# Attention and a Mish layer on one core: weight loads in quarters, deeper input loads, and q/k transposed by DMA instead of TensorE

## The chip, the cores and the metric

The kernel runs on one core of one Trainium2 chip. The metric is the device time of one execution in microseconds (us); lower is better. Before the change it took 547.76 us (median of 3 runs, 545.96 to 547.79; with a fourth run, 547.60). Each run has a granted TensorE clock, the mean share of full speed that the throttle allowed, and a state: "fast" or "slow".

A *slot* in this text is the program's unit of work for one pair of heads: 8 batches of 6 pairs make 48 pairs, 0 to 47.

## The reference, cut to what matters

```python
# q, k, v: (8, 12, 448, 64) f32;  w_in: (768, 2048);  w_out: (2048, 768)
scores = scale * np.matmul(q, k.transpose(0, 1, 3, 2))
m = np.max(scores, axis=-1, keepdims=True)
e = np.exp(scores - m)
attn = e / (np.sum(e, axis=-1, keepdims=True) + np.exp(-m) + 1e-09)   # "softmax off by one"
x = (attn @ v), heads merged                      # 3584 tokens x 768
h = x @ w_in
out = (h * np.tanh(softplus(h))) @ w_out          # Mish between two matrix products
```

## The kernel before

The kernel gives q and k to TensorE with the head dimension on the partitions, so they are transposed. For each pair, SyncE issues seven loads, GpSimd casts to bf16, TensorE transposes against an identity into PSUM, and VectorE copies the result to SBUF. `x_pool` has two PSUM buffers, shared between these transposes and the two attention outputs of a pair.

```python
    stage = ctx.enter_context(tc.tile_pool(name="stage", bufs=3))    # f32 loads, three pairs deep
...
    def transposes(j):
        got = cast.pop(j)
        ps = x_pool.tile([128, 1024], BF16, tag="x", name="tr_ps")
        for i, name in enumerate(("q", "k")):
            mb, tb = got[name]
            for t in range(NT):                                      # NT = 3 blocks of 128 rows
                c = i * S + t * 128
                nc.tensor.transpose(ps[:, c : c + 128], mb[:, t]..., ident)
            c = i * S + MAIN                                         # then the tail of 64 rows
            nc.tensor.transpose(ps[:, c : c + TAIL], tb..., ident[0:64, 0:64])
        qk = work.tile([128, S + MAIN], BF16, tag="qk", name="qk")
        kt = k_tail[j % 2]
        nc.vector.tensor_copy(out=qk, in_=ps[:, 0 : S + MAIN])
        for h in range(2):
            r = slice(h * 64, h * 64 + 64)
            nc.vector.tensor_copy(out=kt[r, r], in_=ps[r, S + MAIN : 2 * S])
        qk_t[j] = qk
```

All weights (12.6 MB of f32, cast to bf16 on the way) are issued by GpSimd at the start. A slot then interleaves the attention of one pair with *units* of the two weight products of earlier batches: `mm1` is x times w_in (6 matmuls a unit), `mm2` is the gated result times w_out (8 matmuls a unit). They fill TensorE while ScalarE works on the softmax. After the fifth slot of a batch, ScalarE does the Mish of the batch before, and eight mm2 units keep TensorE busy meanwhile.

```python
        def slot(j, units):
            ...
            if j + 3 < J:
                load(j + 3)
            if j + 2 < J:
                do_cast(j + 2)
            rest = max(0, len(units) - 2)
            if j < J:
                scores(j, 0)
            take(1)
            if j + 1 < J:
                transposes(j + 1)
            take(1)
            if j >= 1:
                attend(j - 1)
            if j < J:
                scores(j, 1)
            take((rest + 1) // 2)
            if j >= 1:
                normalize(j - 1)
            take(len(units))
```

The softmax here doesn't subtract the row's maximum and nothing guards it: scores larger than these inputs give would overflow.

## Time and profile before

| | before |
|---|---|
| time, median of 3 | 547.76 us |
| span of the profiled execution | 546.4 us |
| TensorE busy, share of the span | 88% |
| ScalarE busy | 55% |
| first Mish starts | 113.0 us |
| last block of eight mm2 units under Mish starts | 463.5 us |

The page of the profiled execution, first its busy times, then busy tenths in 40 slices of 13.7 us (9 is 90% or more; PEclk is the granted clock), then two DMA queues with packets, MB and their share of 16 engines' time. Queue q1 is SyncE's, q0 is GpSimd's, which carries the weights.

```profile
PE 483.3 (88%) x2768; PEld 234.0 (43%) x2768; DVE 206.3 (38%) x414; ACT 297.9 (55%) x419; POOL 130.2 (24%) x400
PE   4354779948999799999999899999997999989996
PEclk9999869986999899999999899999999999989999
DMA  5999554200530434034511353035503420110012
q1 hardware_dynamic: 64768, 44.06, 28.8%
q0 software_dynamic: 2976, 6.29, 6.1%
```

TensorE is little used in the first four slices, where DMA stands at 9 from the second to the fourth, and nearly full from the seventh, but for a dip around the first Mish (slice 9). So the kernel has two regimes with different limits, and the overall 88% describes neither.

The chain of waits of the kernel before (start, length, what) between 14 and 48 us:

```profile
15.95 18.75 DMA km<-in_k_dram
34.76 12.81 DMA kt<-in_k_dram
```

For 31.6 us the chain is nothing but two k loads that queue among the weights. The same view in a slot that TensorE bounds:

```profile
279.77 0.65 PE s_ps L149 x4
280.41 1.24 PE h_ps L205 x6
281.65 0.17 PE tr_ps L125 x3
281.82 0.13 PE tr_ps L129
281.95 0.27 PE tr_ps L125 x3
282.23 0.13 PE tr_ps L129
282.36 1.24 PE h_ps L205 x6
...
287.79 0.33 PE o_ps L248 x2
```

The slot lasts from 279.77 to 287.79, 8.02 us. The four `tr_ps` pieces, the eight transposes of one pair, are 0.70 us of it.

### The profile page before, as it was taken

Reading aid. Unit: us, or ns where it says so; the run is one execution under the profiler, and the core shown is the slowest. Engines: PE = TensorE matmul, PEld = TensorE weight load, DVE = VectorE, ACT = ScalarE, POOL = GpSimd, SP = SyncE. Lnnn points to the kernel's source line nnn. Section 1 sums busy time; section 2 is a strip of 40 time slices with the busy share of each in tenths; the row PEclk is TensorE's granted clock in tenths of the full one; section 3 lists DMA queues with packets and bytes.
Section 4 is the critical chain, followed back from the end, with each engine's and each line's share of the span. In section 5 each row is a group of like instructions: output and inputs, shape, how many; then the busy total and the mean of one; then the engine's idle time right before and its main releaser. Section 6 shows DMA issues by size and latency. Waiting matters only on the chain.

```text
span 546.4 us, 7802 instructions
## 1 busy us (share of the span) xinstructions
PE 483.3 (88%) x2768; PEld 234.0 (43%) x2768; DVE 206.3 (38%) x414; ACT 297.9 (55%) x419; POOL 130.2 (24%) x400
## 2 busy tenths in 40 slices
PE   4354779948999799999999899999997999989996
PEld 1111224413445344555445444554453544535553
DVE  3012224622553245524553255434552365220121
ACT  3034464595567555765658556855577465752200
POOL 5413533230230323112420333013311330000000
PEclk9999869986999899999999899999999999989999
DMA  5999554200530434034511353035503420110012
GB/s 135 212 218 219 149 151 120 67 2 0 138 95 30 130 99 134 1 110 126 152 33 54 106 147 86 31 108 149 134 1 112 120 59 1 59 29 31 29 59 86
DMA packets 67783, 50.85 MB, mean 93 GB/s; under 512 B 24480, under 2 KB 63392, under 8 KB 67744
## 3 DMA queue, kind: packets, MB, share of 16 engines
q1 hardware_dynamic: 64768, 44.06, 28.8%
q0 software_dynamic: 2976, 6.29, 6.1%
q8 instruction: 21, 0.34, 0.3%
q14 instruction: 18, 0.15, 0.1%
HBM read 45.61 MB, written 11.01 MB: 104 GB/s over the span
## 4 chain that ended last, share of the span: by engine, by line
PE 82%; ACT 6%; DMA 6%; SPq 3%; DVE 1%; issue 1%; POOL 0%; POOLq 0%
PE o_ps L248 28%; PE h_ps L205 28%; PE av_ps L172 10%; PE s_ps L149 6%; PE tr_ps L125 4%; DMA km<-in_k_dram 3%; PE av_ps L181 3%; DMA kt<-in_k_dram 2%; PE tr_ps L129 2%; PE s_ps L161 2%; ACT e L156 2%; ACT ln L189 1%; ACT rc L190 1%; SPq L78 1%; ACT gm L233 1%
## 5 line engine op out<-in xcount | busy, mean ns | idle before, releaser
L205 PE MATMUL h_ps<-xT,w_in_sb 128*128 128x448 bf16 x768 | 164.7, 358 | 2.0 <-DVE xT L200 2.0
L189 ACT ACTIVATE ln<-av_ps 64x448 f32<-64x448 f32 x96 | 51.7, 539 | 172.9 <-PE av_ps L181 171.7
L156 ACT ACTIVATE e<-s_ps 128x896 bf16<-128x896 f32 x144 | 126.0, 909 | 22.5 <-PE s_ps L149 20.1
L248 PE MATMUL o_ps<-w_out_sb,gm 128*128 128x384 bf16 x768 | 134.9, 333 | 0.0
L213 DVE COPY h_sb<-h_ps 128x448 f32<-128x448 f32 x112 | 70.0, 625 | 97.0 <-PE h_ps L205 96.1
L205 PEld LDWEIGHTS <-w_in_sb 128*128 128x128 bf16 x768 | 71.2, 99 | 68.4 <-issue 12.0
L248 PEld LDWEIGHTS <-gm 128*128 128x128 bf16 x768 | 75.3, 99 | 53.0 <-issue 5.1
L200 DVE TENSOR_TENSOR xT<-av_ps,rc 64x448 bf16<-64x448 f32 x96 | 59.7, 622 | 74.9 <-ACT rc L190 72.6
L149 PE MATMUL s_ps<-qk 64*128 64x448 bf16 x288 | 52.8, 384 | 27.1 <-ACT e L156 26.1
L256 DVE COPY o_sb<-o_ps 128x384 f32<-128x384 f32 x56 | 31.2, 557 | 100.1 <-PE o_ps L248 99.5
L102 POOL CAST qmb<-qm 128x384 bf16<-128x384 f32 x48 | 24.4, 508 | 141.9 <-DMA qm<-in_q_dram 135.3
L134 DVE COPY qk<-tr_ps 128x832 bf16<-128x832 bf16 x48 | 28.4, 591 | 61.1 <-PE tr_ps L129 58.9
L233 ACT ACTIVATE gm<-h_sb 128x1536 bf16<-128x1536 f32 x28 | 39.2, 1470 | 0.1
L149 PEld LDWEIGHTS <-qk 64*128 64x128 bf16 x288 | 14.5, 96 | 52.2 <-issue 51.0
L125 PE MATMUL tr_ps<-ident,qmb 128*128 128x128 bf16 x144 | 17.9, 240 | 14.5 <-POOL qmb L102 14.5
L190 ACT ACTIVATE rc<-ln 128x448 f32<-128x448 f32 x48 | 27.7, 576 | 1.5
L102 POOL CAST kmb<-km 128x384 bf16<-128x384 f32 x48 | 24.3, 505 | 16.4 <-DMA km<-in_k_dram 16.2
L162 ACT ACTIVATE e<-s_ps 128x448 bf16<-128x448 f32 x48 | 25.7, 536 | 0.0
L125 PE MATMUL tr_ps<-ident,kmb 128*128 128x128 bf16 x144 | 18.1, 242 | 6.5 <-POOL kmb L102 6.5
L125 PEld LDWEIGHTS <-qmb 128*128 128x128 bf16 x144 | 12.2, 106 | 25.8 <-POOL qmb L102 16.1
L248 PE MATMUL o_ps<-w_out_sb,gt 128*128 128x384 bf16 x128 | 22.3, 326 | 0.0
L217 ACT ACTIVATE gm<-h_ps 128x384 bf16<-128x384 f32 x16 | 7.9, 491 | 25.7 <-PE h_ps L205 25.7
(58 smaller groups left out, 338.5 us busy)
## 6 DMA issues: line engine op xcount, KB each, us to landing
qm<-in_q_dram SPq DMA_DIRECT2D x48, 192.0 KB, 2.6
km<-in_k_dram SPq DMA_DIRECT2D x48, 192.0 KB, 2.7
vm<-in_v_dram SPq DMA_DIRECT2D x48, 192.0 KB, 2.7
out_dram<-o_sb SPq DMA_DIRECT2D x24, 384.0 KB, 2.7
w_in_sb<-in_moe_w_in_dram POOLq DMA_DIRECT2D x6, 512.0 KB, 11.5
w_out_sb<-in_moe_w_out_dram POOLq DMA_DIRECT2D x4, 768.0 KB, 26.9
qt<-in_q_dram SPq DMA_DIRECT2D x48, 32.0 KB, 2.6
kt<-in_k_dram SPq DMA_DIRECT2D x48, 32.0 KB, 2.8
```

What stands on the lines that cost most here:

```text
L102: nc.gpsimd.tensor_copy(out=mb.rearrange("p t h d -> p h t d"), in_=main)
L125: nc.tensor.transpose(ps[:, c : c + 128], mb[:, t].rearrange("p h d -> p (h d)"), ident)
L149: nc.tensor.matmul(sp[:, h, 0:S], lhsT=qk[r, S + t * 128 : S + (t + 1) * 128], rhs=qk[r, 0:S], start=True, stop=True,)
L156: nc.scalar.activation(out=e[:, 2 * t : 2 * t + 2, :], in_=sp[:, :, 0:S], func=AF.Exp, scale=SCALE)
L172: nc.tensor.matmul(av[h][:, 0:S], lhsT=va[:, 2 * t + h, :], rhs=e[:, 2 * t + h, :], start=(t == 0), stop=False,)
L189: nc.scalar.activation(out=ln[r, :], in_=av[h][o, 0:S], func=AF.Ln, bias=1.0)
L190: nc.scalar.activation(out=rc, in_=ln, func=AF.Exp, scale=-1.0)
L200: nc.vector.tensor_mul(x_t[b][r, hp, :], av[h][r, 0:S], rc[r, :])
L205: nc.tensor.matmul(hp[:, 0:S], lhsT=w_in_sb[:, dm, ff * 128 : (ff + 1) * 128], rhs=x_t[b][:, dm, :], start=(dm == 0), stop=(dm == DM_T - 1),)
L213: nc.vector.tensor_copy(out=h_sb[:, ff, :], in_=hp[:, 0:S])
L233: nc.scalar.activation(out=gm[:, f, :], in_=h_sb[:, f, 0:MAIN], func=AF.Mish)
L248: nc.tensor.matmul(op[:, 0:HALF], lhsT=lhs, rhs=w_out_sb[:, ff, n * HALF : (n + 1) * HALF], start=(ff == 0), stop=(ff == FF_T - 1),)
```

## The change

Its intent: take q/k transposes off TensorE for pairs 6 to 47, by a DMA that transposes from SBUF to SBUF; and let attention start while the weights come in, by loading them in quarters when slots need them. The rest serves these two: input loads four pairs deep, k and q in one tile (six blocks of 128 rows, then two tails), mm1 and mm2 units placed where TensorE idled. The core of the diff:

```diff
-    stage = ctx.enter_context(tc.tile_pool(name="stage", bufs=3))
+    stage = ctx.enter_context(tc.tile_pool(name="stage", bufs=4))
+    qk_pool = ctx.enter_context(tc.tile_pool(name="qk", bufs=4))
...
     def do_cast(j):
...
+        if j >= NPAIR:                      # NPAIR = 6
+            qk = qk_pool.tile([128, 2 * S], BF16, tag="qk", name="qk")
+            nc.sync.dma_start_transpose(
+                out=qk[:, 0 : 2 * MAIN].rearrange("p (t c) -> p t c", c=128),
+                in_=mb.rearrange("p t h d -> p (t h d)"),
+            )
+            nc.sync.dma_start_transpose(
+                out=qk[:, 2 * MAIN : 2 * S].rearrange("p (t c) -> p t c", c=TAIL),
+                in_=tb.rearrange("p t h d -> p (t h d)"),
+            )
+            qk_t[j] = qk
...
     def transposes(j):
+        if j >= NPAIR:
+            for h in range(2):
+                r = slice(h * 64, h * 64 + 64)
+                nc.gpsimd.tensor_copy(out=kt[r, r], in_=qk_t[j][r, S + MAIN : 2 * S])
+            return
+        for t in range(2 * NT):             # six blocks of 128 rows
+            nc.tensor.transpose(...)
+        for t in range(2):                  # then both tails
+            nc.tensor.transpose(...)
...
-        for dm in range(DM_T):              # all weights at the start
-            nc.gpsimd.dma_start(out=w_in_sb[:, dm, :], ...)
+        def load_w_in(i):                   # a quarter of the columns of w_in
+            c = slice(i * d_ff // 4, (i + 1) * d_ff // 4)
+            nc.gpsimd.dma_start(
+                out=w_in_sb[:, :, c], in_=moe_w_in[:, c].rearrange("(m p) f -> p m f", p=128)
+            )
...
-            if j + 3 < J:
-                load(j + 3)
+            if j + 4 < J:
+                load(j + 4)
             if j + 2 < J:
                 do_cast(j + 2)              # the DMA transposes are issued in here
+            if 1 <= j <= 4:
+                load_w_in(j - 1)
+            if 6 <= j <= 9:
+                load_w_out(j - 6)
...
+                late = p == 1 and i == 0    # two mm1 units at the end of slot 6
...
-        slot(J, [])
+        m2 = mm2_units(B - 2)
+        slot(J, m2[:4])                     # four mm2 units in the last slot
+        m2 = m2[4:]
```

More of the change, by code (lines that the diff above doesn't have):

```diff
@@ L97, in do_cast @@
         tiles = loaded.pop(j)
-        got = {}
-        for name in ("q", "k"):
+        mb = half.tile([128, 2 * NT, 2, D], BF16, tag="mb", name="mb")
+        tb = half.tile([64, 2, 2, D], BF16, tag="tb", name="tb")
+        for i, name in enumerate(("k", "q")):
             main, tail = tiles[name]
-            mb = half.tile([128, NT, 2, D], BF16, tag=f"{name}mb", name=f"{name}mb")
-            nc.gpsimd.tensor_copy(out=mb.rearrange("p t h d -> p h t d"), in_=main)
-            tb = half.tile([64, 2, D], BF16, tag=f"{name}tb", name=f"{name}tb")
-            nc.gpsimd.tensor_copy(out=tb, in_=tail)
-            got[name] = (mb, tb)
+            nc.gpsimd.tensor_copy(
+                out=mb[:, i * NT : (i + 1) * NT].rearrange("p t h d -> p h t d"), in_=main
+            )
+            nc.gpsimd.tensor_copy(out=tb[:, 1 - i], in_=tail)
         main, tail = tiles["v"]
@@ L115, in do_cast @@
             )
-        cast[j] = got
-    def transposes(j):
-        got = cast.pop(j)
-        ps = x_pool.tile([128, 1024], BF16, tag="x", name="tr_ps")
-        for i, name in enumerate(("q", "k")):
-            mb, tb = got[name]
-            for t in range(NT):
-                c = i * S + t * 128
-                nc.tensor.transpose(
-                    ps[:, c : c + 128], mb[:, t].rearrange("p h d -> p (h d)"), ident
-                )
-            c = i * S + MAIN
+        cast[j] = (mb, tb)
+        if j >= NPAIR:
[9 more added lines that the diff above has]
+            qk_t[j] = qk
+    def transposes(j):
+        mb, tb = cast.pop(j)
+        kt = k_tail[j % 2]
+        if j >= NPAIR:
[3 more added lines that the diff above has]
+            return
+        ps = x_pool.tile([128, 1024], BF16, tag="x", name="tr_ps")
+        for t in range(2 * NT):
             nc.tensor.transpose(
-                ps[:, c : c + TAIL], tb.rearrange("p h d -> p (h d)"), ident[0:64, 0:64]
+                ps[:, t * 128 : (t + 1) * 128], mb[:, t].rearrange("p h d -> p (h d)"), ident
             )
-        qk = work.tile([128, S + MAIN], BF16, tag="qk", name="qk")
-        kt = k_tail[j % 2]
-        nc.vector.tensor_copy(out=qk, in_=ps[:, 0 : S + MAIN])
+        for t in range(2):
+            c = 2 * MAIN + t * TAIL
+            nc.tensor.transpose(
+                ps[:, c : c + TAIL], tb[:, t].rearrange("p h d -> p (h d)"), ident[0:64, 0:64]
+            )
+        qk = qk_pool.tile([128, 2 * S], BF16, tag="qk", name="qk")
+        nc.vector.tensor_copy(out=qk[:, 0 : S + MAIN], in_=ps[:, 0 : S + MAIN])
         for h in range(2):
@@ L150, in scores @@
                     sp[:, h, 0:S],
-                    lhsT=qk[r, S + t * 128 : S + (t + 1) * 128],
-                    rhs=qk[r, 0:S],
+                    lhsT=qk[r, t * 128 : (t + 1) * 128],
+                    rhs=qk[r, MAIN : MAIN + S],
                     start=True,
@@ L160, in scores @@
             sp = s_pool.tile([128, 2, 512], FP32, tag="s", name="s_ps")
-            nc.tensor.matmul(sp[:, 0, 0:S], lhsT=kt, rhs=qk[:, 0:S], start=True, stop=True)
+            nc.tensor.matmul(sp[:, 0, 0:S], lhsT=kt, rhs=qk[:, MAIN : MAIN + S], start=True, stop=True)
             nc.scalar.activation(
@@ L280 @@
         nc.scalar.preload_act_table_set("natural_log_exp_and_others")
-        for j in range(3):
+        for j in range(4):
             load(j)
@@ L285, with load_w_out, slot, take @@
         do_cast(1)
-        for dm in range(DM_T):
+        def load_w_in(i):
+            c = slice(i * d_ff // 4, (i + 1) * d_ff // 4)
             nc.gpsimd.dma_start(
-                out=w_in_sb[:, dm, :], in_=moe_w_in[dm * 128 : (dm + 1) * 128, :]
+                out=w_in_sb[:, :, c], in_=moe_w_in[:, c].rearrange("(m p) f -> p m f", p=128)
             )
-        n = FF_T // 4
-        for i in range(4):
-            f = slice(i * n * 128, (i + 1) * n * 128)
+        def load_w_out(i):
+            n = FF_T // 4
             nc.gpsimd.dma_start(
                 out=w_out_sb[:, i * n : (i + 1) * n, :],
-                in_=moe_w_out[f, :].rearrange("(f p) c -> p f c", p=128),
-            )
-        def slot(j, units):
-            def take(n):
+                in_=moe_w_out[i * n * 128 : (i + 1) * n * 128, :].rearrange(
+                    "(f p) c -> p f c", p=128
+                ),
+            )
+        def slot(j, units, late=False):
+            def take(n, last=False):
+                if late and not last:
+                    return
                 for _ in range(min(n, len(units))):
                     units.pop(0)()
-            if j + 3 < J:
-                load(j + 3)
+            if j + 4 < J:
+                load(j + 4)
             if j + 2 < J:
                 do_cast(j + 2)
+            if 1 <= j <= 4:
+                load_w_in(j - 1)
+            if 6 <= j <= 9:
+                load_w_out(j - 6)
             rest = max(0, len(units) - 2)
@@ L320, in slot @@
                 normalize(j - 1)
-            take(len(units))
+            take(len(units), last=True)
         for p in range(B):
@@ L326 @@
             for i in range(NPAIR):
-                if i == 0:
+                late = p == 1 and i == 0
+                if late:
+                    units, m1 = m1[:2], m1[2:]
+                elif i == 0:
                     units, m2 = m2[:4], m2[4:]
@@ L332 @@
                     units, m2 = m2, []
-                slot(p * NPAIR + i, units)
+                slot(p * NPAIR + i, units, late)
                 if i == 4 and p >= 1:
@@ L338 @@
                         u()
-        slot(J, [])
+        m2 = mm2_units(B - 2)
+        slot(J, m2[:4])
+        m2 = m2[4:]
         m1 = mm1_units(B - 1, direct=True)
-        m2 = mm2_units(B - 2)
         while m1 or m2:
```

## The prediction

> **What bounds the kernel now (547.8 us; profiled span 546.4).** Three regimes, by the chain of waits and the table by stretches.
>
> 1. 0 to 79.5 us, pairs 0 to 6, no weight matmuls yet. From 16 to 48 us the DMA engines are saturated (share 1.11, 219 GB/s) by all weights, issued from 11.7 us on. They cost 6.1% of 16 engines' span, 33 us of full DMA time, and q/k/v loads queue behind them: the chain shows 18.75 us of `km` and 12.81 us of `kt`. Attention starts at 24.6, 37.6, 49.3, then every 8.2 us once the weights are in: a latency loop (scores, transposes, VectorE copy, attention, Ln, Exp) at a granted clock of 0.69.
> 2. 79.5 to 487 us: TensorE almost without gaps. In a full slot the eight transposes take 0.70 us of the chain.
> 3. In slots without filler (around the first Mish, and near 300, 418 and 480 us) TensorE waits on ScalarE; transposes plus the VectorE copies that release the second PSUM buffer cost about 2 us there. After the last attention TensorE waits 3 us (483.2 to 486.3).
>
> **What the change does.**
> - Weights: quarters issued in slots 1 to 4 and 6 to 9. A quarter is 33/8 = 4.2 us of DMA, a pair's loads 2.9 us (0.37 of 32 us for four pairs). 7.1 us fits in 8.2 us, so slots 1 to 6 should run at their latency. Estimate: slot 7 starts at 61 us, not 79.5: minus 18.
> - Transposes: 40 slots lose 0.70 us each: minus 28; unfilled slots lose 2 us: another 3.5. VectorE loses 42 copies of 591 ns and 84 of 184 ns; GpSimd (24% busy) gains 84 of some 0.2 us.
> - Two mm1 units (1.24 us each) fill idle time in slot 6: minus 2. Four mm2 units in the last slot: minus 2.6.
> - Added: two DMA transposes per pair on SyncE's queue, where seven load issues take 4.55 us. No trace here has a DMA transpose; the Trainium skill ("DMA: Bandwidth & Descriptors", Latency and other measured facts) gives 261 GB/s, so 230 KB are about 1 us of data, an estimate; issue I guess at 1 to 2 us each. That makes 6.5 to 8.5 us of queue per 7.3 us slot, below the batch mean of 9. They are issued about two slots before their scores, so latencies up to 8 us hide. The same page (Rules for kernel authors) says a transpose next to ordinary DMAs needs nothing.
>
> Sum: 18 + 31.5 + 4.6 = 54. I give back 1 us, and 6 more for contention in slots 1 to 10 and for stores that block SyncE ahead of transposes: **about 494 us**, range 481 to 512. Chances: faster by over 2% 0.95, within 2% 0.03, slower 0.02.
>
> **What would show each step.** The chain has no `km`/`kt` DMA pieces over 10 us; the first h_ps matmul comes at 52 to 64 us; DMA share is below 1 in slots 1 to 4. From slot 7 TensorE stays 95% busy, full slots last 7.3 instead of 8.0 us, and no TensorE wait names `qk` or `k_tail` released by a DMA. Six slots last about 54 instead of 58.6 us.
>
> **What would make it wrong.** DMA transposes that cost over 3 us each of SyncE's queue or over 8 us to land (scores then wait on `qk`, and slots follow the queue); w_out quarters plus transposes saturating the DMA in slots 6 to 9; weight quarters arriving after their mm1; ScalarE, 58% busy in full slots, becoming the limit.

## The result, and the profile after

The changed kernel takes 494.84 us (median of 4 runs, 491.99 to 498.20), against 547.60 us for the kernel before: a ratio of 0.9045, 95% interval 0.8969 to 0.9120. Ratios here and below are the mean time of one kernel's fast runs over that of the other's of the same rounds, so they are not quite the ratios of the medians. Executions over 1.5% slower than the fastest of the same kernel are left out of the means. All four runs fall in two groups, 492.0 and 492.3 at clocks of 0.965 and 0.960, and 497.4 and 498.2 at 0.947 and 0.943. The profiled run is the 497.4, so its trace shows the slower of the two groups, about 2.5 us above the median; what separates the groups, no trace here shows.

The page of the changed kernel, the same lines as before, and the shares of the chain of waits by engine:

```profile
PE 441.5 (89%) x2432; PEld 209.9 (42%) x2432; DVE 169.6 (34%) x288; ACT 297.9 (60%) x419; POOL 144.6 (29%) x482
PE   3677595828999899999998999999998999999995
PEclk9956697977999999999999999999999999999999
DMA  5699999951543464446453564365544620120112
q1 hardware_dynamic: 105088, 53.71, 42.8%
q0 software_dynamic: 5248, 6.29, 8.2%
PE 80%; DMA 7%; ACT 6%; SPq 3%; POOL 1%; issue 1%; DVE 0%; POOLq 0%
```

Three things stand out. The start is busier (TensorE row, slices 2 to 4), though slices 5 and 7 fall back to 5 tenths. The high DMA load now lasts to the eighth slice, about 99 us. And the weights, the same 12.6 MB, cost 8.2% of 495.6 us, 40.6 us of full DMA time, where they cost 6.1% of 546.4, 33.3 us, before. They come in 5,248 packets, not 2,976, because quarters of w_in's columns are cut into pieces of 1,024 bytes, not 4,096. But this is only half of it: by the packets in the two traces, w_in rose from 15.8 to 19.8 us, and w_out from 17.2 to 20.8 with the same 2,048 packets of 1,536 bytes. Why these took longer in slots 6 to 9, no run separates.

A full slot on the chain of waits of the changed kernel:

```profile
243.87 0.65 PE s_ps L165 x4
244.52 2.38 PE h_ps L221 x12
...
251.08 0.62 PE s_ps L165 x3
```

It lasts 7.21 us, 0.81 less: the 0.70 us of transposes are gone, and the two mm1 units that stood around them run without a break, in 2.38 us where they took 1.24 twice. VectorE's copies and their wait are gone as well.

Where the time came from, by three marks in the two profiled executions:

| mark | before | after | saved up to here |
|---|---|---|---|
| first Mish starts | 113.0 | 99.3 | 13.7 |
| last block of eight mm2 units under Mish starts | 463.5 | 416.2 | 47.3 |
| end | 546.4 | 495.6 | 50.8 |

So 13.7 us come from the first 11 slots, 33.6 from the next 36, most of which TensorE bounds, and 3.5 from the end.

But the first part is less than it should be. Scores of pair 7 start at 62.3 us in place of 79.1, 16.8 us earlier; by the first Mish, only 13.7 us are left, although four slots without transposes on TensorE lie between. The waits view (who waited for whom: us in total, times, longest) names what took it back:

```profile
PE s_ps L165 <- DMA qk<-tb: 9.4, 3, 5.2
PEld L165 <- DMA qk<-mb: 9.3, 2, 5.6
```

These are matmuls and their weight loads, waiting for transposes by DMA. In the timeline, the longest of them, with the issue of the transpose that it waited for:

```profile
71.18 1.18 SPq L125 DMA_TRANSPOSE qk<-tb  x1
...
81.81 0.93 PE L165 MATMUL s_ps<-qk 64*128 64x448 bf16 x4 [5.22 <-DMA qk<-tb]
```

This transpose landed 10.5 us after its issue; over the whole run the medians in the DMA issues view are 2.8 us (`qk<-mb`) and 2.3 (`qk<-tb`). It was also issued late: TensorE was ready for it at 76.6, only 5.4 us after its issue, although it stands two slots ahead in the program. And the wait cost more than its 5.2 us: the twelve h_ps matmuls after it took 4.66 us, where twelve take 2.43 just before the wait, at a granted clock of 0.50 from 81.8 to 87.4 us.

Busy time by stretches in the changed kernel, 32 to 48 and 62 to 82 us. The columns are stretch, length, busy time of TensorE, its weight loads, VectorE, ScalarE and GpSimd with counts, then granted clock, mean busy share of the DMA engines and GB/s. A share is the sum of the packets' times over the stretch, so it can exceed 1.

```profile
32.00:48.00 16.00, 11.31 (x43) 3.64 (x43) 3.76 (x10) 9.24 (x14) 7.38 (x22) 0.61 1.17 223
62.00:82.00 20.00, 14.51 (x80) 6.47 (x82) 7.50 (x13) 9.24 (x14) 7.37 (x23) 0.98 1.13 192
```

The DMA engines are saturated in both, in the second with TensorE idle for over a quarter of the time.

A second reading matters for what follows. SyncE's queue in a full slot of the changed kernel (start, length of the issue, line, what):

```profile
194.33 0.57 SPq L79 DMA_DIRECT2D qm<-in_q_dram  x1
194.96 0.66 SPq L91 DMA_DIRECT2D qt<-in_q_dram  x1
195.66 0.59 SPq L79 DMA_DIRECT2D km<-in_k_dram  x1
196.30 0.63 SPq L91 DMA_DIRECT2D kt<-in_k_dram  x1
196.97 0.59 SPq L79 DMA_DIRECT2D vm<-in_v_dram  x1
197.61 1.13 SPq L86 DMA_DIRECT2D vt<-in_v_dram  x2
198.85 1.25 SPq L121 DMA_TRANSPOSE qk<-mb  x1
200.20 1.17 SPq L125 DMA_TRANSPOSE qk<-tb  x1
201.43 0.57 SPq L79 DMA_DIRECT2D qm<-in_q_dram  x1
```

Nine issues take 7.10 us, back to back, in a slot of 7.21 us. In these slots the queue is full.

### The profile page after: what moved, and what is told of

The parts are those of the page before. It is cut to its first block, busy times and chain, and to the rows that moved or that the text cites. A ratio compares the mean times of both kernels' runs of the same rounds, so it can differ in the third digit from the quotient of the medians.

```text
span 495.6 us, 7105 instructions
## 1 busy us (share of the span) xinstructions
PE 441.5 (89%) x2432; PEld 209.9 (42%) x2432; DVE 169.6 (34%) x288; ACT 297.9 (60%) x419; POOL 144.6 (29%) x482
## 3 DMA queue, kind: packets, MB, share of 16 engines
q1 hardware_dynamic: 105088, 53.71, 42.8%
q0 software_dynamic: 5248, 6.29, 8.2%
## 4 chain that ended last, share of the span: by engine, by line
PE 80%; DMA 7%; ACT 6%; SPq 3%; POOL 1%; issue 1%; DVE 0%; POOLq 0%
PE o_ps L264 30%; PE h_ps L221 29%; PE av_ps L188 10%; PE s_ps L165 6%; DMA qk<-tb 3%; PE av_ps L197 3%; PE s_ps L177 2%; DMA vm<-in_v_dram 2%; ACT e L172 1%; ACT ln L205 1%; ACT gm L249 1%; DMA km<-in_k_dram 1%; DMA vt<-in_v_dram 1%; SPq L79 1%; ACT rc L206 1%
## 5 line engine op out<-in xcount | busy, mean ns | idle before, releaser
L221 PE MATMUL h_ps<-xT,w_in_sb 128*128 128x448 bf16 x768 | 158.6, 356 | 1.4 <-DVE xT L216 1.4
L264 PE MATMUL o_ps<-w_out_sb,gm 128*128 128x384 bf16 x768 | 132.0, 330 | 0.0
L221 PEld LDWEIGHTS <-w_in_sb 128*128 128x128 bf16 x768 | 73.4, 99 | 72.3 <-issue 11.2
L137 POOL COPY k_tail_97<-qk 64x64 bf16<-64x64 bf16 x42 | 9.8, 234 | 112.9 <-DMA qk<-tb 72.3
L137 POOL COPY k_tail_95<-qk 64x64 bf16<-64x64 bf16 x42 | 9.8, 234 | 76.3 <-DMA qk<-tb 48.2
L104 POOL CAST mb<-km 128x384 bf16<-128x384 f32 x48 | 24.2, 503 | 19.8 <-DMA km<-in_k_dram 17.2
L104 POOL CAST mb<-qm 128x384 bf16<-128x384 f32 x48 | 24.2, 503 | 0.0
L188 PE MATMUL av_ps<-e,v_aug_89 128*128 128x448 bf16 x72 | 18.0, 389 | 0.5 <-DVE k_tail_97 L153 0.5
L188 PE MATMUL av_ps<-e,v_aug_87 128*128 128x448 bf16 x72 | 18.0, 389 | 0.5 <-DVE k_tail_95 L153 0.5
```

Source lines behind the costliest of these rows:

```text
L104: nc.gpsimd.tensor_copy(out=mb[:, i * NT : (i + 1) * NT].rearrange("p t h d -> p h t d"), in_=main)
L188: nc.tensor.matmul(av[h][:, 0:S], lhsT=va[:, 2 * t + h, :], rhs=e[:, 2 * t + h, :], start=(t == 0), stop=False,)
L221: nc.tensor.matmul(hp[:, 0:S], lhsT=w_in_sb[:, dm, ff * 128 : (ff + 1) * 128], rhs=x_t[b][:, dm, :], start=(dm == 0), stop=(dm == DM_T - 1),)
L264: nc.tensor.matmul(op[:, 0:HALF], lhsT=lhs, rhs=w_out_sb[:, ff, n * HALF : (n + 1) * HALF], start=(ff == 0), stop=(ff == FF_T - 1),)
```

## The experiments

The total was as predicted, so the question is whether its parts were. The theory: (a) the start and the transposes are separate gains; (b) the first 11 slots lose some 8 us to a DMA overload; (c) SyncE's queue just keeps up. Rivals stand in each expectation.

### 1. The two halves alone

Weights, depth and fillers alone, every pair transposed by TensorE:

```diff
-        if j >= NPAIR:       # both places
+        if j >= J:
```

> Weight quarters, 4-deep loads and fillers, but every pair transposed by TensorE. Theory (the start and the transposes are two separate gains): slot 7 starts near 62 us as in the changed kernel, no TensorE wait names a DMA of qk, and each of the 42 pairs pays 0.8 to 1.0 us again: about 525 us, 20 to 25 us faster than before. Rival (the gain is nearly all transposes; early weight loading was hidden anyway): within 8 us of before, 540 or more.

Measured: 519.07 us, ratio 0.9512 (0.9456 to 0.9568). It is 6 us faster than expected. Slot 7 starts at 62.4 us, as expected. First Mish starts at 93.8 us, earlier than in the whole change (99.3), and no TensorE wait names a DMA of qk.

DMA transposes alone, with weights early, three-deep loads and no fillers, as in the kernel before:

```diff
-    stage = ctx.enter_context(tc.tile_pool(name="stage", bufs=4))
+    stage = ctx.enter_context(tc.tile_pool(name="stage", bufs=3))
...
-            if j + 4 < J:
-                load(j + 4)
+            if j + 3 < J:
+                load(j + 3)
...      (all weight loads ahead of slot 0; no "late" units; slot(J, []))
```

> DMA transposes of pairs 6 to 47 alone; weights early, loads 3-deep, no fillers, as before. Theory: slot 7 starts near 79 us as before, then about 1 us less per slot, 36 to 38 us in all: about 510 us. Rival (DMA transposes only pay with deeper loads, because SyncE's queue has no slack left): over 520 us, with TensorE or GpSimd waiting on loads or on qk in the full slots.

Measured: 506.23 us, ratio 0.9268 (0.9217 to 0.9318). Also faster than expected, and the rival falls: the transposes pay without deeper loads. Slot 7 starts at 74.0 us, not near 79 as expected, and the first Mish at 104.8 against 113.0. In the contended window of the other runs, 40 to 100 us, no transpose here took over 2.9 us to land.

The two ratios save 4.9% and 7.3%, together 12.2% or 66.8 us of 547.5. The whole change saves 9.55% or 52.3 us. So 14.5 us are lost when the two are put together, give or take some 6 us by the three intervals, and the next runs look for them.

### 2. A gain that was counted twice: the order of TensorE's transposes

The weights-only run had an unexpected detail. Its transposes take 0.50 us of a slot, not 0.70, although they are the same eight. The diff had also regrouped them: six blocks, then two tails. So this was done alone, in the kernel before:

```diff
         for i, name in enumerate(("q", "k")):
             mb, tb = got[name]
             for t in range(NT):
                 nc.tensor.transpose(...)        # three of 128 rows
+        for i, name in enumerate(("q", "k")):
+            mb, tb = got[name]
             c = i * S + MAIN
             nc.tensor.transpose(...)            # the tail of 64 rows
```

> The kernel before with one thing changed: a pair's eight TensorE transposes in the order six of 128 rows, then two of 64, not 3 + 1 + 3 + 1. The weights-only run shows 0.50 us of the chain for them, against 0.70 before. Theory: 0.20 us in each of some 40 slots that TensorE bounds: 8 us, 539 us. Rival (the 0.20 us came from the other edits of that run): within 2 us of before.

Measured: 537.70 us, ratio 0.9829 (0.9806 to 0.9852): 9.4 us from splitting one loop. A piece of its chain of waits:

```profile
257.53 1.24 PE h_ps L207 x6
258.77 0.34 PE tr_ps L125 x6
259.11 0.16 PE tr_ps L131 x2
259.27 1.24 PE h_ps L207 x6
```

Six take 0.34 us, where two groups of three took 0.17 and 0.27 before: the three blocks that followed a tail of 64 rows had cost 0.10 us more than the three that did not. The other 0.10 us comes from the tails, 0.16 us for both together where each took 0.13 alone. Why a change of shape costs TensorE this, no run here shows.

This gain is part of the weights-only run and cannot be had again once the transposes have left TensorE. It explains about 9 of the missing 14.5 us.

### 3. The overload of the first slots

By the queue shares, a quarter of the weights costs 40.6/8 = 5.1 us of full DMA time; a pair's loads 2.5 us; a pair's transposes (42.8% of 495.6 minus 28.8% of 546.4, over 42 pairs) 1.3 us. In slots 6 to 9 that makes 8.9 us in slots of 7.2 us. The loads are put here at the rate of q1 before the change, 44.06 MB in 28.8% of 546.4 us, 280 GB/s; the 2.9 us of the prediction and of an expectation below counts in an output store that ran in the same 32 us. Five runs attack this from different sides.

Loads three pairs deep again, all else as changed:

```diff
-            if j + 4 < J:
-                load(j + 4)
+            if j + 3 < J:
+                load(j + 3)
...      (stage bufs=3, three loads ahead of slot 0)
```

> The changed kernel with loads 3 deep instead of 4. Theory (depth only covers the longer landing times while weights are in flight): 2 to 8 us slower than the changed kernel, all lost before 110 us, full slots still 7.2 us. Rival (depth is what made the start faster): 12 us or more slower.

Measured: 490.94 us, ratio 0.8992 (0.8937 to 0.9047). Both theory and rival fail: it is not slower. First Mish starts at 90.6 us, 8.8 us earlier than in the changed kernel. Deeper loads do not help here.

The w_out quarters further apart:

```diff
-            if 6 <= j <= 9:
-                load_w_out(j - 6)
+            if j in (6, 8, 10, 11):
+                load_w_out((6, 8, 10, 11).index(j))
```

> The changed kernel with the w_out quarters in slots 6, 8, 10 and 11 instead of 6 to 9. Theory (5.1 us for a quarter plus 2.9 us of loads plus 1.3 us of transposes exceed a 7.2 us slot in slots 6 to 9): the 5.2 us wait of TensorE for qk at 82 us goes, first Mish near 93 us instead of 99, 5 to 8 us faster, near 488 us. Rival (the wait comes from the order of issue or from SyncE's queue, not from bytes): within 2 us of the changed kernel.

Measured: 491.74 us, ratio 0.9003 (0.8953 to 0.9052). This is 2 to 3 us better, inside the intervals, and less than expected. Where the theory looked it was right: pair 9 waits 0.6 us instead of 5.2, and the first Mish starts at 93.3 us. But TensorE's matmuls still wait 10.1 us in all for transposes, in other places, 3.8 us at 54 and 4.2 at 95. Fewer bytes per slot cure the wait they were aimed at, not the rest.

Four-deep loads kept, but each slot's transposes issued ahead of its loads:

```diff
-            if j + 4 < J:
-                load(j + 4)
             if j + 2 < J:
                 do_cast(j + 2)
+            if j + 4 < J:
+                load(j + 4)
```

> The changed kernel (4-deep loads) with each slot's two DMA transposes issued before its loads, not after them. On SyncE's queue this gives exactly the order of the 3-deep run, with the deeper buffers kept. Theory (a transpose lands late because one more pair of loads stands ahead of it in the queue): the 5.2 us wait on qk at 82 us goes, time within 3 us of the 3-deep run, near 490 us, and no slower. Rival (3-deep was better for another reason, such as fewer bytes in flight): within 2 us of the changed kernel, 494 us.

Measured: 489.72 us, ratio 0.8945 (0.8923 to 0.8967), a time as the theory said; the first Mish starts at 92.9 us. The wait got shorter and did not go, as the waits view shows:

```profile
PE s_ps L165 <- DMA qk<-tb: 5.2, 3, 2.7
PEld L165 <- DMA qk<-mb: 7.2, 3, 3.0
```

Between 40 and 100 us a transpose still landed up to 11.1 us after its issue, but was issued earlier, pair 6's at 39.9 us instead of 47.6. On SyncE's queue this order, T(j+2) L(j+4) T(j+3) L(j+5), is the same as the three-deep one, L(j+3) T(j+2) L(j+4) T(j+3), so depth as such is not what differs. In the order of the change, one more pair of loads stands ahead of each transpose, loads that nobody needs yet, and part of that time TensorE waits. Times alone are weak evidence here: the interval of this run and that of the changed kernel (0.8969 to 0.9120) only just part, and the three-deep run's overlaps both.

The two cures together:

> Transposes ahead of loads in each slot, and the w_out quarters in slots 6, 8, 10 and 11. Theory: the two cures act on the same wait, so they don't add: 1 to 3 us faster than transposes-first alone, 487 to 489 us, first Mish near 90 us. Rival (they add up, 2.6 and 5 us): 484 us or less.

Measured: 488.03 us, ratio 0.8934 (0.8911 to 0.8957). All four runs lie within 0.5 us, where the changed kernel's spread over 6 us. First Mish starts at 88.5 us, and no matmul waits for qk any more (3.9 us of weight-load waits remain). Stretch 62 to 82 us of this run, with the columns as above:

```profile
62.00:82.00 20.00, 20.00 (x110) 8.73 (x109) 10.07 (x18) 12.69 (x20) 9.39 (x31) 1.00 0.86 175
```

TensorE has no gap at all where it was busy 14.5 of 20 us, and DMA is below saturation. Whether the two cures add, the times do not tell: it is about 1 us over the order alone, within the intervals, and a full sum, 2 to 3 us more, would have given 487 us (the 484 of the rival counts more than that). In the profiled executions they nearly add: against 99.3 us, the first Mish starts 6.0 us earlier with the quarters spread, 6.4 with the order changed, 10.8 with both.

Last, no DMA transposes while w_out loads, by leaving pairs 6 to 11 to TensorE:

```diff
-        if j >= NPAIR:       # both places
+        if j >= 12:
```

> The changed kernel with pairs 6 to 11 transposed by TensorE too, so that no DMA transpose is in flight with the w_out quarters. Theory: six slots pay 0.6 us again in filled slots and about 2 us where nothing fills (some 5 us), and the waits on qk before 100 us (about 9 us of TensorE, and the low clock after) go: first Mish near 94 us as in the weights-only run, 488 to 492 us. Rival (waits on qk cost little in the end): slower than the changed kernel by 4 us or more.

Measured: 492.84 us, ratio 0.9013 (0.8992 to 0.9034). First Mish starts at 94.6 us, as in the weights-only run, and no TensorE wait for a DMA of qk is left. What it gains on waits it pays in transposes: the two nearly cancel. It ends just outside the range expected, 2 us from the changed kernel and inside its interval.

With this the sum closes, within the intervals. The halves save 66.8 us; minus the 9.4 us of regrouping counted twice, 57.4 us. Transposes first saves 57.8 us (1 minus 0.8945, of 547.5), with the spread quarters 58.4. The change as given saves 52.3; the remaining 5 to 6 us are what the crowded start costs, through the order of the queue and the bytes in it together. Their shares are not shown.

### 4. How full is SyncE's queue?

Each pair's two DMA transposes issued twice, the second time into a tile that is never read (the results stay correct):

```diff
+            qk2 = qk_pool.tile([128, 2 * S], BF16, tag="qk2", name="qk2")
+            nc.sync.dma_start_transpose(out=qk2[:, 0 : 2 * MAIN]..., in_=mb...)
+            nc.sync.dma_start_transpose(out=qk2[:, 2 * MAIN : 2 * S]..., in_=tb...)
             qk_t[j] = qk
```

> The changed kernel with each pair's two DMA transposes issued twice, the second pair into tiles that nobody reads. Full slots keep SyncE's queue busy 7.0 to 7.1 us (4.6 for seven loads, 2.4 for two transposes) of TensorE's 7.2. Theory (the queue is as good as full, it only keeps up): full slots become 9.4 to 9.6 us long, TensorE waits on qk, and the time rises by 30 to 50 us, to 525 to 545 us. Rival (the queue has slack, or the engines that move the bytes set the pace): under 10 us more.

Measured: 555.50 us, ratio 1.0146 (1.0111 to 1.0181), slower than even the kernel before and 61 us slower than the changed one: the theory in kind, above its range in size. The chain of waits by engine, on this run's page:

```profile
PE 48%; SPq 33%; DMA 8%; ACT 5%; issue 3%; DVE 1%; POOL 1%; POOLq 0%
```

and two successive first transposes on SyncE's queue:

```profile
267.21 1.25 SPq L121 DMA_TRANSPOSE qk<-mb  x1
...
276.92 1.25 SPq L121 DMA_TRANSPOSE qk<-mb  x1
```

A slot now takes 9.71 us, the queue's time, and a third of the chain is SyncE issuing. The engines that move the bytes are not the limit: the DMA share is 0.54 in the stretch from 400 to 450 us. From the first Mish (105.5 us) to the last (476.2) a batch of six slots takes 61.8 us, six times 9.71 and 3.5 more, so the slots with Mish gave nothing back either.

### 5. The fillers

Without the two mm1 units in slot 6 and the four mm2 units in the last slot:

```diff
-                late = p == 1 and i == 0
+                late = False
...
-        m2 = mm2_units(B - 2)
-        slot(J, m2[:4])
-        m2 = m2[4:]
+        slot(J, [])
+        m2 = mm2_units(B - 2)
```

> The changed kernel without its two fillers: no mm1 units in slot 6, no mm2 units in the last slot. Theory (as predicted): the 3 us wait of TensorE after the last attention returns, and 2.5 us of mm1 move from the idle end of slot 6 into bound slots: 4 to 5 us slower than the changed kernel, 499 us. Rival (the two mm1 units land in the phase that waits on transposes anyway, so only the end counts): 2 to 3 us slower.

Measured: two of four runs were slow (547.08 at a clock of 0.817, 503.42); the profiled one is among them, so it has no stage times to compare. The two fast runs are 495.93 and 496.70, ratio 0.9086 (0.9049 to 0.9123), 2.2 us above the changed kernel and inside both intervals. So the fillers may be worth about 2 us, as the rival said, but this run doesn't show it.

### 6. A further idea that failed

In every second batch, the slot after Mish has no filler, and TensorE waits there. Two of the eight mm2 units under Mish were moved into it, on top of transposes first:

```diff
-                    first, m2 = m2[:8], m2[8:]
+                    n = 6 if len(m2) == 8 else 8
+                    first, m2 = m2[:n], m2[n:]
```

> Transposes first, and in every second batch six mm2 units under Mish and two in the slot after it, which had none. Theory: in that slot ScalarE idled 1.34 us and TensorE waited for it; 1.2 us in each of three batches: 3 to 4 us faster than transposes-first alone, near 486 us. Rival (TensorE then waits under Mish instead): no gain.

Measured: 488.54 us, ratio 0.8952 (0.8905 to 0.9000), no gain over transposes first (0.8945). The chain of waits of this run suggests why:

```profile
249.29 7.80 PE o_ps L264 x48
257.09 0.48 PE s_ps L165 x4
257.57 2.71 PE o_ps L264 x16
260.28 1.14 PE av_ps L188 x6
...
261.75 0.53 ACT ln L205
```

The slot takes its first two units (`o_ps` x16) ahead of the attention (`av_ps`), so they only delay it, and ScalarE's Ln after it. They would have to stand behind it; this was not tried.

The same split with three-deep loads and spread w_out quarters:

> 3-deep loads, w_out quarters in slots 6, 8, 10 and 11, and the 6 + 2 split. Same order on SyncE's queue as transposes first. Theory: as the sum of the two runs above, 484 to 487 us, the fastest of all.

Measured: 487.80 us, ratio 0.8925 (0.8897 to 0.8954), just above the range expected. It cannot be told apart from transposes first plus spread quarters (0.8934), since the split gives nothing. Both beat the changed kernel by a bit over 1%, just clear of its wide interval.

## Why the prediction was right, point by point

The time was predicted at 494 us, in a range of 481 to 512, and measured at 494.84. The parts were less exact than the sum.

- **The start: right in size, wrong in one reason.** "Slot 7 starts at 61 us": 62.3. But "a quarter is 33/8 = 4.2 us of DMA" is mis-sized: the quarters cost 5.1 us each, and about half of the rise is that w_out's unchanged packets took longer. The 2.9 us for a pair's loads erred the other way; they take 2.5. "DMA share is below 1 in slots 1 to 4" failed, at 1.17 from 32 to 48 us. "From slot 7 TensorE stays 95% busy" failed too at first: 80% from 62.3 to 99.3 us, and 95% from there to 430.
- **Transposes off TensorE: right, somewhat small.** Full slots were to last 7.3 us and last 7.21. The step "40 slots lose 0.70 us each" is low by 0.1 us a slot, since the matmuls around the transposes also run closer. Six slots were to last 54 instead of 58.6 us; from the marks at 152.1 and 416.2 us in the changed kernel (five batches) they last 52.8, and 58.8 before (169.4 to 463.5). The prediction did not see that 0.20 of the 0.70 us came from the order of the transposes, not from their being on TensorE.
- **"No TensorE wait names qk or k_tail released by a DMA": wrong.** Matmuls wait 9.4 us for `qk<-tb`. The prediction did name the overload of slots 6 to 9 among what would make it wrong, and set aside 6 us for contention in slots 1 to 10. The whole of it costs 5 to 6 us by the transposes-first and the combined run. The step that failed is "issued about two slots before their scores, so latencies up to 8 us hide": the longest wait is for a transpose that left 5.4 us before TensorE was ready and took 10.5 to land. What it did not see is that the order of issue matters as well as the bytes.
- **SyncE's queue: right in size.** 6.5 to 8.5 us of issues per slot were predicted; it is 7.1 us, 1.25 and 1.17 us for the two transposes. Doubling them shows how close this is to the limit.
- **The bytes of a transpose.** An estimate of 1 us of data stood on 261 GB/s from the Trainium skill, "DMA: Bandwidth & Descriptors", section Latency and other measured facts. Here 229,376 bytes take 1.3 us of all 16 engines, 176 GB/s, by the difference of two queue shares.
- **The fillers: not shown.** Predicted 4.6 us, 2.2 us by two fast runs, inside the noise. The wait after the last attention was also smaller than read: in the timeline of the kernel before, five mm1 matmuls ran inside it, and TensorE's idle time was 2.05 us, not 3.
- **ScalarE did not become the limit.** Its share of the chain of waits is 6%, as before.

So an allowance for contention, the mis-sized weight quarters and a low figure per slot offset each other. The range was right for reasons that mostly held; the closeness of 494 and 494.84 is partly luck. No run took 494.84 us: it is the middle of two groups, near 492 and 498.

## What to carry to other kernels

Work moved from a full engine to DMA puts its latency into a queue: look at what stands ahead of it in program order, and issue what is needed next before what is needed later, or deeper prefetch can make the needed transfer late. Count the issue time of a queue per iteration against the iteration's length before adding to it; here 7.1 of 7.2 us were used, and 2.4 us more would have undone the whole gain. When a diff regroups instructions on the way, test that alone: here it gave 9 us that looked like part of something else.

## What the Trainium skill lacked or had wrong

- "DMA: Bandwidth & Descriptors", Latency and other measured facts, gives 261 GB/s for a DMA transpose with a non-contiguous middle dimension. Whether that is this case, no run shows. From SBUF to SBUF with 239-byte packets on average (9.65 MB more in 40,320 more packets), it was 176 GB/s of full DMA time: 229,376 bytes in 1.3 us.
- "Advanced Engine Details and Errata", X-Bar Transpose (TRN2), says that transpose DMAs are as fast as regular DMAs. Here queue q1 moved 280 GB/s before the change, with loads and stores alone, so the transposes, at 176, were over a third slower per byte. Part of this is the size of the packets: the loads' own packets of 256 bytes took 18.2 ns each before the change, the transposes' packets of 256 bytes 21 to 22 in three runs. Neither page gives the issue time of a DMA transpose on its queue in us (the first has sequencer cycles, in its part on trn3): 1.25 us for 128 x 768 and 1.17 us for 64 x 256, against 0.57 to 0.66 us for a load.
- "DMA: Bandwidth & Descriptors", Issuing engines are not separate DMA queues, calls the sequencer's issue time "usually small relative to the DMA itself". In this kernel seven loads take 4.5 us to issue and 2.5 us of full DMA time, and the issuing queue became the limit in the doubled run (9.71 us a slot) at a DMA share of 0.54.
- The same page, Rules for kernel authors, says a transpose next to ordinary DMAs needs nothing. For correct results this held in every run; of time the row says nothing, and there it mattered: beside weight loads a transpose landed up to 11.5 us after its issue, in place of a median of 2.8.
- "TensorE: Matmul & The Clock Gate", Part 4: PE-mode transpose, gives about 275 ns for one in a kernel's context. Pipelined, six of 128 x 128 took 0.34 us of the chain, 57 ns each. No page gives a cost in time for alternating 128-row and 64-row transposes: a pair's eight took 0.70 us in the order 3 + 1 + 3 + 1, 0.50 us in the order 6 + 2.
